# Windowed attention with sinks and a highway layer: x transposed by TensorE one block behind, weights loaded early, another order of the engines' work

## Chip, cores and metric

The kernel runs on one core of a Trainium2 chip. The metric is the device time of one execution in microseconds. The profile is one profiled execution of the kernel; its span runs from the first to the last instruction, and the execution's time is a little longer than the span.

## What is computed

Sliding-window attention that also keeps four sink positions, then a highway layer on its output:

```
scores = q k^T / sqrt(64)                 # 4 batches, 8 heads, 768 positions
keep   = (position < 4) or (0 <= i - j < 128)
a      = softmax(scores where keep)
x      = (a v), heads side by side        # 3072 tokens x 512
H      = max(x w_h, 0)
T      = sigmoid(x w_t + b_t)
out    = T H + (1 - T) x                  # 3072 x 512, float32
```

The inputs and the output are float32 in memory; the kernel computes in float16 with float32 accumulation.

## The kernel before, in words

**Tiling.** The 3072 tokens are 24 blocks of 128, six to a batch. A block sees its own 128 keys, those of the block before it in its batch, and the batch's four sinks. Block n goes through these steps, each a small function:

- `load_qk`, `load_v` (L79, L88): q, k, v of the block for all eight heads, by DMAs that GpSimd issues and that convert to float16.
- `pe_T`, `act_T`: TensorE transposes q and k (eight transposes into one PSUM tile `tp`), ScalarE copies them to SBUF (`qk`).
- `pe_S`, `act_S`, `dve_mask`: scores in two groups of four heads (g = 0 and 1), ScalarE's exponential (`e`), VectorE's product with the mask.
- `pe_sink`, `act_sink`: for two blocks at a time, the scores against the sinks and their exponential (`es`).
- `pe_A`: attention times v into one PSUM tile `av`; a column of v holds the softmax denominator. `dve_rec`, `dve_x`: its reciprocal and x (`xh`).
- x transposed, either by TensorE with a copy by ScalarE (`pe_X`, `act_X`) or by a DMA that SyncE issues (`sp_X`), into `xT`.
- the highway: `pe_Mt` (bias and x w_t, five matmuls), `act_u` (tanh), `pe_Mh` (x w_h, four matmuls), then VectorE's `dve_d`, `dve_e`, `dve_o` (`dd`, `ee`, `otok`), and SyncE's store of the block's 256 KB.

**Order.** No scheduler moves anything: the order of the calls in one loop is the order on each engine. Iteration i computes the attention product of block i, the scores of block i + 1, the transposes of block i + 2, the loads of block i + 10, x's transpose by TensorE of block i - 1 (for blocks up to 14; from 15 on SyncE's DMA, issued as soon as x is there), and the highway of block m = i - 4 (LAG is 4), whose VectorE part, o = i - 5, follows one iteration later. After block 23's attention the loop therefore runs on with highways alone. An engine that waits at one of its instructions holds all that stand behind it.

**PSUM.** The tag "m" has two buffers, taken in turn by `tp`, `xtp`, `tps`, `hps` and `sk`. The order of these in the loop decides which one's reader must be done before the next may be written: in the old order `tps` takes the buffer of `tp`, and `hps` that of `xtp`.

**Buffers in SBUF.** q, k have eight, v a ring of twelve. x and its transpose have LAG + 3 = 7.

**GpSimd's queue.** It issues the loads of blocks 0 to 2 and builds the masks, then the load of the first batch's four sink values of v (`load_sink_v(0)`), then, in iteration -2, copies the sinks' keys (`pool_sink`), spreads the sinks' values over a block-diagonal tile (`sink_v`, a product that waits for that load), and issues blocks 3 to 8, with the highway's weights behind blocks 4 and 5. For each later batch `pool_sink` and `sink_v` stand where its first block has been transposed.

Of the kernel before, what the change touches and what calls it, by code (L numbers as in the profile page):

```python
# [20 lines left out]
def kernel(  # L21
# [18 lines left out]
    nc = tc.nc  # L40
    P = 128

    B, H, S, D = q.shape
    NSINK = int(n_sink)
# [7 lines left out]
    NSC = S // P  # L52
    assert NSC % 2 == 0
    NB = NT // P
    NHP = H // 2
# [1 line left out]
    SCALE = 1.0 / math.sqrt(D)  # L57
    VW = H * 65 + 64
    AHEAD = 8
    LAG = 4  # L60
    WAT = 4

    const = ctx.enter_context(tc.tile_pool(name="const", bufs=1))
    sd_pool = ctx.enter_context(tc.tile_pool(name="p_sd", bufs=AHEAD))
    qkT_pool = ctx.enter_context(tc.tile_pool(name="p_qkT", bufs=5))
    e_pool = ctx.enter_context(tc.tile_pool(name="p_e", bufs=5))
    r_pool = ctx.enter_context(tc.tile_pool(name="p_r", bufs=3))
    x_pool = ctx.enter_context(tc.tile_pool(name="p_x", bufs=LAG + 3))
    td_pool = ctx.enter_context(tc.tile_pool(name="p_td", bufs=3))
    o_pool = ctx.enter_context(tc.tile_pool(name="p_o", bufs=4))  # L70
    s_ps = ctx.enter_context(tc.tile_pool(name="ps_s", bufs=2, space=bass.MemoryType.PSUM))
# [1 line left out]
    m_ps = ctx.enter_context(tc.tile_pool(name="ps_m", bufs=2, space=bass.MemoryType.PSUM))  # L73

    NV = AHEAD + 4
    v_ring = [const.tile([P, VW], FP16, tag=f"v{i}", name=f"v{i}") for i in range(NV)]
    qk_sd = {}

    def load_qk(n):  # L79
        b, c = divmod(n, NSC)  # L80
        rows = slice(c * P, (c + 1) * P)
        qsd = sd_pool.tile([P, H, D], FP16, tag="qsd", name="qsd")
        ksd = sd_pool.tile([P, H, D], FP16, tag="ksd", name="ksd")
        nc.gpsimd.dma_start(out=qsd, in_=q[b, :, rows, :].transpose([1, 0, 2]))  # L84
        nc.gpsimd.dma_start(out=ksd, in_=k[b, :, rows, :].transpose([1, 0, 2]))  # L85
        qk_sd[n] = (qsd, ksd)

    def load_v(n):  # L88
# [16 lines left out]
    wh_sb = const.tile([P, NOC, DM], FP16, tag="wh")  # L105
    wt_sb = const.tile([P, NOC, DM], FP16, tag="wt")
    bt32 = const.tile([1, DM], FP32, tag="bt32")
    bt16 = const.tile([P, DM], FP16, tag="bt16")
    ones_row = const.tile([P, P], FP16, tag="ones_row")
    NS4 = H * 4  # L110
    KW = NHP * P + 32
    ks_bd = [const.tile([P, KW], FP16, tag=f"ks{i}", name=f"ks{i}") for i in range(2)]
    vs_bd = [const.tile([P, H, 65], FP16, tag=f"vs{i}", name=f"vs{i}") for i in range(2)]
    vs_dn = [const.tile([NS4, D], FP16, tag=f"vd{i}", name=f"vd{i}") for i in range(2)]
# [9 lines left out]
            init_v(vt)  # L124

    def load_sink_v(b):
        nc.gpsimd.dma_start(out=vs_dn[b % 2], in_=v[b, :, 0:4, :])

    def sink_v(b):
        nc.gpsimd.tensor_tensor(  # L130
            out=vs_bd[b % 2][0:NS4, :, 0:D], in0=vs_dn[b % 2].unsqueeze(1).to_broadcast([NS4, H, D]),
            in1=bm[0:NS4, :].unsqueeze(2).to_broadcast([NS4, H, D]), op=ALU.mult)

    with tc.manual_schedule(engines={ENG.Pool}):
        load_qk(0)
        nc.gpsimd.affine_select(
            out=ident, in_=ident, compare_op=ALU.is_equal, fill=0.0,
            base=0, pattern=[[-1, P]], channel_multiplier=1)
        load_v(0)
        load_qk(1)  # L140
        nc.gpsimd.affine_select(
            out=mask[:, 1, :], in_=mask[:, 1, :], compare_op=ALU.is_ge, fill=0.0,
            base=0, pattern=[[1, P]], channel_multiplier=-1)
        load_v(1)
        nc.gpsimd.affine_select(
            out=mask[:, 0, :], in_=mask[:, 0, :], compare_op=ALU.is_ge, fill=0.0,
            base=-1, pattern=[[-1, P]], channel_multiplier=1)
        load_qk(2)
        nc.gpsimd.affine_select(
            out=bm, in_=bm, compare_op=ALU.is_ge, fill=0.0,  # L150
            base=0, pattern=[[-4, H]], channel_multiplier=1)
        nc.gpsimd.affine_select(
            out=bm, in_=bm, compare_op=ALU.is_ge, fill=0.0,
            base=3, pattern=[[4, H]], channel_multiplier=-1)
        load_v(2)
        load_sink_v(0)

    nc.sync.dma_start(out=bt32, in_=moe_b_t.unsqueeze(0))

    def more_constants():  # L160
# [3 lines left out]
        for i in range(2):  # L164
            nc.vector.memset(ks_bd[i], 0.0)
            nc.vector.memset(vs_bd[i], 0.0)
            nc.vector.memset(es_t[i], 0.0)

    def late_constants():
        nc.vector.tensor_copy(out=mask0, in_=mask[:, 1, :])  # L170
        nc.vector.memset(mask0[0:NSINK, :], 1.0)
        nc.vector.tensor_copy(out=mask1, in_=mask)
        nc.vector.memset(mask1[0:NSINK, 0, :], 1.0)
        nc.vector.tensor_scalar_mul(bt16[0:1, :], bt32, 0.5)

    def sink_ones():
        for i in range(2):
            nc.vector.tensor_scalar_mul(vs_bd[i][0:NS4, :, D:D + 1],
                                        bm[0:NS4, :].unsqueeze(2), 2.0)

# [3 lines left out]
            nc.tensor.matmul(w, lhsT=warm[:, 0:P], rhs=warm, start=True, stop=True)  # L184

    qkT, tp_of, s_of, e_of, av_of, rec_of = {}, {}, {}, {}, {}, {}
    xtp_of = {}
    xh_of, xT_of, t_of, u_of, h_of, dd_of, ee_of, sk_of = {}, {}, {}, {}, {}, {}, {}, {}

    def pe_T(n):  # L190
        qsd, ksd = qk_sd.pop(n)
# [7 lines left out]
    def act_T(n):  # L199
        qk = qkT_pool.tile([P, 2 * NHP, P], FP16, tag="qk", name="qk")  # L200
        nc.scalar.copy(out=qk, in_=tp_of.pop(n))  # L201
        qkT[n] = (qk[:, 0:NHP, :], qk[:, NHP:2 * NHP, :])

    def pool_sink(b):
        _, kT = qkT[b * NSC]
        ks = ks_bd[b % 2]
        for hh in range(2):
            rows = slice(64 * hh, 64 * hh + 64)
            dst = ks[rows, 0:NHP * 136].rearrange("p (a b) -> p a b", b=136)
            nc.gpsimd.tensor_copy(out=dst[:, :, 4 * hh:4 * hh + NSINK],  # L210
                                  in_=kT[rows, :, 0:NSINK])

    def pe_sink(n):
# [124 lines left out]
    def dve_d(n):  # L338
        dd = td_pool.tile([P, DM], FP16, tag="dd", name="dd")
        nc.vector.scalar_tensor_tensor(out=dd, in0=h_of.pop(n), scalar=0.0, in1=xh_of[n],  # L340
                                       op0=ALU.max, op1=ALU.subtract)
        dd_of[n] = dd
# [10 lines left out]
                                       op0=ALU.mult, op1=ALU.add)  # L353
        nc.sync.dma_start(out=out[n * P:(n + 1) * P, :], in_=otok)

    def by_dma(n):
        return n >= 15

    def on(n):
        return 0 <= n < NB  # L360

    with tc.manual_schedule(engines={ENG.PE, ENG.DVE, ENG.Activation, ENG.SP, ENG.Pool}):
        for i in range(-2, NB + LAG + 1):
            m, o = i - LAG, i - LAG - 1
            if i == -2:
                warm_up(8)
                more_constants()
                late_constants()
                sink_ones()
            if on(i) and i % NSC >= 2 and i % 2 == 0:  # L370
                act_sink(i)
            if on(i + 1):
                pe_S(i + 1, 0)
                act_S(i + 1, 0)
                pe_S(i + 1, 1)
            if on(o):
                dve_d(o)
            if on(i):
                dve_mask(i, 1)
            if on(i + 2):  # L380
                pe_T(i + 2)
            if on(i - 1) and not by_dma(i - 1):
                pe_X(i - 1)
            if on(o):
                dve_e(o)
            if on(i):
                pe_A(i)
            if on(i + 2):
                act_T(i + 2)
            if on(i - 1) and not by_dma(i - 1):  # L390
                act_X(i - 1)
            if on(i + 1):
                act_S(i + 1, 1)
                dve_mask(i + 1, 0)
            if on(i):
                dve_rec(i)
            if on(o):
                dve_o(o)
            if on(i):
                dve_x(i)  # L400
                if by_dma(i):
                    sp_X(i)
            if on(m):
                pe_Mt(m)
                act_u(m)
                pe_Mh(m)
            if on(i + 1) and (i + 1) % NSC >= 2 and (i + 1) % 2 == 0:
                pe_sink(i + 1)
            if on(i + 2) and (i + 2) % NSC == 0:
                pool_sink((i + 2) // NSC)  # L410
                sink_v((i + 2) // NSC)
            for n in (range(3, AHEAD + 1) if i == -2 else [i + 2 + AHEAD]):
                if n < NB:
                    load_qk(n)
                    load_v(n)
                if n == WAT:
                    nc.gpsimd.dma_start(out=wt_sb, in_=moe_w_t.rearrange("(kc p) of -> p kc of", p=P))
                if n == WAT + 1:
                    nc.gpsimd.dma_start(out=wh_sb, in_=moe_w_h.rearrange("(kc p) of -> p kc of", p=P))
            b = i // NSC + 1  # L420
            if i >= 0 and i % NSC == 1 and b < B:
                load_sink_v(b)


# [33 lines left out]
```

The softmax here doesn't subtract the row's maximum and nothing guards it: scores larger than these inputs give would overflow.

## Time and profile before

| what | us |
|---|---|
| median of 8 runs (lowest, highest) | 140.16 (138.28, 141.6) |
| the profiled execution | 139.09 |
| its span | 137.4 |
| TensorE busy | 114.0 |
| VectorE busy | 98.2 |
| ScalarE busy | 94.1 |
| GpSimd busy | 74.9 |
| start of the attention product of blocks 1, 2, 3, 4, 5 | 21.36, 26.07, 30.87, 35.96, 40.10 |
| first highway matmul | 37.00 |
| last attention product ends | 120.6 |
| last store issued | 133.47 |

How to read it: PE is TensorE's matmuls, PEld its weight loads, DVE is VectorE, ACT ScalarE, POOL GpSimd, SP SyncE. A group of instructions is named by its line, engine and operation, then the tile it writes, an arrow, and the tiles it reads. Busy time on TensorE is rough, since matmuls overlap and their ends are modelled: a matmul of 512 columns shows 379 ns while the next starts after 215 ns. "Idle before" is the time an engine stood before an instruction, with what released it. The chain of waits follows the work that ended last back to its beginning.

### The profile page before, as it was taken

The page shows a single profiled execution, that of the slowest core. Times are in us where ns is not written, and L with a number is a line of the kernel's source. Part 1 is how long each engine was busy: PE and PEld are TensorE (multiplying, and loading weights), DVE is VectorE, ACT ScalarE, POOL GpSimd, SP SyncE. Part 2 cuts the span into 40 slices and gives each one's busy share as a digit, 9 for nine tenths or more (in the row PEclk, how much of TensorE's full clock was granted, in tenths as well). Part 3 has the DMA queues.
Part 4 walks back from the last instruction along what each step waited for, and adds up shares of the span by engine and source line. Part 5 has one row for each costly group of instructions (what it writes and reads, how often), then busy time and mean ns, then how long its engine had stood idle before and what let it go on. Part 6 is the DMA issues. An engine that isn't in the chain of part 4 may idle for free.

```text
span 137.4 us, 3217 instructions
## 1 busy us (share of the span) xinstructions
PE 114.0 (83%) x1276; PEld 73.7 (54%) x1276; DVE 98.2 (72%) x213; ACT 94.1 (68%) x120; POOL 74.9 (55%) x99
## 2 busy tenths in 40 slices
PE   6747419946799799999997999999999999799910
PEld 2226319835676367567664675676655777354300
DVE  6434602364378697788789977978899988979970
ACT  3048807859687897897879878978697987413300
POOL 6994899955999949997799995005000000000000
PEclk9985555699999999999999999999999999999997
DMA  0999099999999999999999999943233243333322
GB/s 5 111 126 103 5 111 142 143 177 173 156 154 157 196 198 183 141 169 196 190 179 162 174 173 170 166 117 115 93 105 94 58 119 115 99 109 102 127 102 79
DMA packets 84626, 18.19 MB, mean 132 GB/s; under 512 B 80514, under 2 KB 81538, under 8 KB 84611
## 3 DMA queue, kind: packets, MB, share of 16 engines
q0 software_dynamic: 76256, 10.51, 113.5%
q1 hardware_dynamic: 8354, 7.48, 16.7%
q8 instruction: 10, 0.16, 0.5%
q14 instruction: 6, 0.04, 0.1%
HBM read 21.01 MB, written 6.29 MB: 199 GB/s over the span
## 4 chain that ended last, share of the span: by engine, by line
PE 44%; ACT 17%; POOL 15%; DMA 9%; DVE 8%; issue 3%; POOLq 0%; DVEq 0%
PE hps L334 11%; PE tps L321 11%; ACT e L249 9%; ACT qk L201 7%; DMA ksd<-in_k_dram 7%; PE av L275 5%; POOL qsd L84 5%; PE sps L241 4%; PE tps L319 4%; POOL ksd L85 4%; POOL v L92 4%; DVE dd L340 3%; DVE ee L346 3%; DVE otok L352 3%; PE sk L219 2%
## 5 line engine op out<-in xcount | busy, mean ns | idle before, releaser
L249 ACT ACTIVATE e<-sps,ebias 128x1024 f16<-128x1024 f32 (+1 forms) x48 | 49.8, 1045 | 6.4 <-PE sps L241 6.2
L260 DVE TENSOR_TENSOR e<-e,mask 128x1024 f16<-128x1024 f16 (+1 forms) x48 | 31.0, 646 | 5.5 <-ACT e L249 5.1
L201 ACT COPY qk<-tp 128x1024 f16<-128x1024 f16 x24 | 24.1, 1004 | 14.1 <-PE tp L196 14.1
L275 PE MATMUL av<-v,e 128*128 128x112 f16 x352 | 24.7, 219 | 0.8 <-DVE e L260 0.8
L340 DVE SCALAR_TENSOR_TENSOR dd<-hps,xh 128x512 f16<-128x512 f32 x24 | 16.6, 690 | 11.8 <-PE hps L334 11.7
L334 PE MATMUL hps<-wh_sb,xT 128*128 128x512 f16 x96 | 24.6, 379 | 0.0
L321 PE MATMUL tps<-wt_sb,xT 128*128 128x512 f16 x96 | 24.6, 379 | 0.0
L84 POOL DMA_DIRECT2D qsd<-in_q_dram x24 | 22.3, 928 | 3.6 <-DMA wt_sb<-in_moe_w_t_dram 1.6
L85 POOL DMA_DIRECT2D ksd<-in_k_dram x24 | 21.9, 912 | 2.3 <-DMA wh_sb<-in_moe_w_h_dram 1.5
L92 POOL DMA_DIRECT2D v<-in_v_dram x24 | 21.9, 912 | 2.0 <-DMA ksd<-in_k_dram 1.4
L275 PEld LDWEIGHTS <-e 128*128 128x128 f16 x352 | 21.3, 101 | 1.9 <-DVE e L260 1.2
L327 ACT ACTIVATE u<-tps 128x512 f16<-128x512 f32 x24 | 14.5, 603 | 10.6 <-PE tps L321 10.6
L241 PE MATMUL sps<-qk 64*128 64x128 f16 x352 | 15.9, 229 | 4.3 <-ACT qk L201 2.6
L346 DVE SCALAR_TENSOR_TENSOR ee<-u,dd 128x512 f16<-128x512 f16 x24 | 17.3, 721 | 0.5
L241 PEld LDWEIGHTS <-qk 64*128 64x128 f16 x352 | 11.1, 99 | 11.5 <-issue 9.5
L294 DVE TENSOR_TENSOR xh<-av,rec 128x512 f16<-128x512 f32 x24 | 16.4, 684 | 0.2
L321 PEld LDWEIGHTS <-xT 128*128 128x128 f16 x96 | 9.3, 97 | 13.0 <-issue 3.9
L352 DVE SCALAR_TENSOR_TENSOR otok<-xh,ee 128x512 f32<-128x512 f16 x24 | 15.6, 652 | 0.2
L334 PEld LDWEIGHTS <-xT 128*128 128x128 f16 x96 | 9.4, 98 | 11.8 <-issue 0.8
L194 PE MATMUL tp<-ident,qsd 128*128 128x128 f16 x96 | 10.4, 236 | 4.5 <-DMA qsd<-in_q_dram 4.5
L289 DVE RECIPROCAL rec<-av 128x8 f32<-128x8 f32 x24 | 4.9, 204 | 11.7 <-PE av L275 6.3
L196 PE MATMUL tp<-ident,ksd 128*128 128x128 f16 x96 | 10.2, 234 | 3.4 <-DMA ksd<-in_k_dram 3.4
(48 smaller groups left out, 93.7 us busy)
## 6 DMA issues: line engine op xcount, KB each, us to landing
out_dram<-otok SPq DMA_DIRECT2D x24, 256.0 KB, 2.6
qsd<-in_q_dram POOLq DMA_DIRECT2D x24, 128.0 KB, 6.8
ksd<-in_k_dram POOLq DMA_DIRECT2D x24, 128.0 KB, 6.7
v<-in_v_dram POOLq DMA_DIRECT2D x24, 128.0 KB, 6.6
wt_sb<-in_moe_w_t_dram POOLq DMA_DIRECT2D x1, 512.0 KB, 8.1
wh_sb<-in_moe_w_h_dram POOLq DMA_DIRECT2D x1, 512.0 KB, 9.9
xT<-xh SPq DMA_TRANSPOSE x9, 2.4
vd<-in_v_dram POOLq DMA_DIRECT2D x4, 4.0 KB, 7.0
```

The costliest lines, as they stand in the source:

```text
L84: nc.gpsimd.dma_start(out=qsd, in_=q[b, :, rows, :].transpose([1, 0, 2]))
L85: nc.gpsimd.dma_start(out=ksd, in_=k[b, :, rows, :].transpose([1, 0, 2]))
L92: nc.gpsimd.dma_start(out=vt[:, :, 0:D], in_=v[b, :, rows, :].transpose([1, 0, 2]))
L201: nc.scalar.copy(out=qk, in_=tp_of.pop(n))
L241: nc.tensor.matmul(sps[:, hh, o:o + P], lhsT=kk[rows, hp, :], rhs=qT[rows, hp, :], start=True, stop=True)
L249: nc.scalar.activation(out=e.rearrange("p a b c d -> p a (b c d)"), in_=sps[:, :, 0:2 * np_ * P], func=AF.Exp, bias=ebias, scale=SCALE)
L260: nc.vector.tensor_tensor(out=ev, in0=ev, in1=m.unsqueeze(1).to_broadcast([P, 4, np_ * P]), op=ALU.mult)
L275: nc.tensor.matmul(av[:, g, 2 * hl + hh, 0:_AVN], lhsT=e[:, hh, hl, pc, :], rhs=vt[:, 65 * h:65 * h + _AVN], start=first, stop=False, skip ...
L321: nc.tensor.matmul(tps, lhsT=xT[:, kc, :], rhs=wt_sb[:, kc, :], start=False, stop=(kc == NOC - 1))
L334: nc.tensor.matmul(hps, lhsT=xT[:, kc, :], rhs=wh_sb[:, kc, :], start=(kc == 0), stop=(kc == NOC - 1))
L340: nc.vector.scalar_tensor_tensor(out=dd, in0=h_of.pop(n), scalar=0.0, in1=xh_of[n], op0=ALU.max, op1=ALU.subtract)
L346: nc.vector.scalar_tensor_tensor(out=ee, in0=u_of.pop(n), scalar=1.0, in1=dd_of.pop(n), op0=ALU.add, op1=ALU.mult)
```

## The change

- x of every block but 14 to 21 is transposed by TensorE (before: blocks 0 to 14), in the iteration after its attention; blocks 14 to 21 by SyncE's DMA.
- The highway of a block runs one iteration after its attention, or two where the DMA transposes it. Iteration 15 has none, iteration 23 has two (21 and 22). The loop ends two iterations after the last block instead of five.
- Inside an iteration, x's transpose and ScalarE's copy of it come directly behind the next block's scores; ScalarE's copy of q, k follows, ahead of the exponential of the second score group.
- The first iterations (-2 to 1) have an order of their own: scores and transposes are put at the end of the iteration, and the highway of block 0 ahead of the transposes of block 2.
- GpSimd issues the weights behind v of block 1, ahead of q, k of block 2. The sinks' values of batch 0 are spread by VectorE in iteration 0; those of later batches by GpSimd, with the load issued a batch ahead.
- x and its transpose have five buffers.

The diff, cut to its core:

```diff
-    LAG = 4
-    WAT = 4
...
-    x_pool = ctx.enter_context(tc.tile_pool(name="p_x", bufs=LAG + 3))
+    x_pool = ctx.enter_context(tc.tile_pool(name="p_x", bufs=5))
...
+    XBAR = range(14, 22)
...
-    def sink_v(b):
-        nc.gpsimd.tensor_tensor(
+    def sink_v(b, eng):
+        eng.tensor_tensor(
...
+    def load_w(w, sb):
+        nc.gpsimd.dma_start(out=sb, in_=w.rearrange("(kc p) of -> p kc of", p=P))
...
-        load_v(1)
         nc.gpsimd.affine_select(
             out=mask[:, 0, :], in_=mask[:, 0, :], compare_op=ALU.is_ge, fill=0.0,
             base=-1, pattern=[[-1, P]], channel_multiplier=1)
-        load_qk(2)
+        load_v(1)
+        load_sink_v(0)
+        load_w(moe_w_t, wt_sb)
+        load_w(moe_w_h, wh_sb)
...
+        load_qk(2)
         load_v(2)
-        load_sink_v(0)
+        load_qk(3)
...
-    def by_dma(n):
-        return n >= 15
+    def lag(n):
+        return 2 if n in XBAR else 1
+
+    def highway(i):
+        return [m for m in range(NB) if m + lag(m) == i]
+
+    def has_sink(n):
+        return on(n) and n % NSC >= 2 and n % 2 == 0
...
-        for i in range(-2, NB + LAG + 1):
-            m, o = i - LAG, i - LAG - 1
+        for i in range(-2, NB + 2):
+            ms, os_ = highway(i), highway(i - 1)
             if i == -2:
                 warm_up(8)
                 more_constants()
-                late_constants()
-                sink_ones()
...
-            if on(i + 1):
+            if i >= 2 and on(i + 1):
                 pe_S(i + 1, 0)
                 act_S(i + 1, 0)
                 pe_S(i + 1, 1)
-            if on(o):
-                dve_d(o)
+            if on(i - 1) and i - 1 not in XBAR:
+                pe_X(i - 1)
+                act_X(i - 1)
+            for o in os_:
+                if o not in dd_of:
+                    dve_d(o)
             if on(i):
                 dve_mask(i, 1)
-            if on(i + 2):
+            if i >= 2 and on(i + 2):
                 pe_T(i + 2)
-            if on(i - 1) and not by_dma(i - 1):
-                pe_X(i - 1)
-            if on(o):
+                act_T(i + 2)
+            if i >= 2 and on(i + 1):
+                act_S(i + 1, 1)
+            for o in os_:
                 dve_e(o)
             if on(i):
                 pe_A(i)
-            if on(i + 2):
-                act_T(i + 2)
-            if on(i - 1) and not by_dma(i - 1):
-                act_X(i - 1)
-            if on(i + 1):
-                act_S(i + 1, 1)
+            if i >= 2 and on(i + 1):
                 dve_mask(i + 1, 0)
             if on(i):
                 dve_rec(i)
-            if on(o):
+            for o in os_:
                 dve_o(o)
             if on(i):
                 dve_x(i)
-                if by_dma(i):
+                if i in XBAR:
                     sp_X(i)
-            if on(m):
+            for m in ms:
                 pe_Mt(m)
                 act_u(m)
                 pe_Mh(m)
-            if on(i + 1) and (i + 1) % NSC >= 2 and (i + 1) % 2 == 0:
+            if i == 1:
+                dve_d(0)
+                pe_T(2)
+                act_T(2)
+            if -1 <= i < 2:
+                for g in range(2):
+                    pe_S(i + 1, g)
+                    act_S(i + 1, g)
+                dve_mask(i + 1, 0)
+            if i < 2:
+                n = {-2: 0, -1: 1, 1: 3}.get(i)
+                if n is not None:
+                    pe_T(n)
+                    act_T(n)
+            if has_sink(i + 1):
                 pe_sink(i + 1)
+            if i == 0:
+                sink_ones()
+                sink_v(0, nc.vector)
             if on(i + 2) and (i + 2) % NSC == 0:
-                pool_sink((i + 2) // NSC)
-                sink_v((i + 2) // NSC)
-            for n in (range(3, AHEAD + 1) if i == -2 else [i + 2 + AHEAD]):
+                b = (i + 2) // NSC
+                pool_sink(b)
+                if b:
+                    sink_v(b, nc.gpsimd)
+                if b + 1 < B:
+                    load_sink_v(b + 1)
+            for n in {-2: range(3, AHEAD + 1), 0: [], 1: [10, 11]}.get(i, [i + 2 + AHEAD]):
                 if n < NB:
-                    load_qk(n)
+                    if n > 3:
+                        load_qk(n)
                     load_v(n)
-                if n == WAT:
-                    nc.gpsimd.dma_start(out=wt_sb, in_=moe_w_t.rearrange("(kc p) of -> p kc of", p=P))
-                if n == WAT + 1:
-                    nc.gpsimd.dma_start(out=wh_sb, in_=moe_w_h.rearrange("(kc p) of -> p kc of", p=P))
-            b = i // NSC + 1
-            if i >= 0 and i % NSC == 1 and b < B:
-                load_sink_v(b)
```

More of the change, by code (lines that the diff above doesn't have):

```diff
@@ L75 @@
     NV = AHEAD + 4
+    NS4 = H * NSINK
+    KW = NHP * P + 32
+    XBAR = range(14, 22)
     v_ring = [const.tile([P, VW], FP16, tag=f"v{i}", name=f"v{i}") for i in range(NV)]
@@ L109 @@
     ones_row = const.tile([P, P], FP16, tag="ones_row")
-    NS4 = H * 4
-    KW = NHP * P + 32
     ks_bd = [const.tile([P, KW], FP16, tag=f"ks{i}", name=f"ks{i}") for i in range(2)]
@@ L126, in load_sink_v @@
     def load_sink_v(b):
-        nc.gpsimd.dma_start(out=vs_dn[b % 2], in_=v[b, :, 0:4, :])
-    def sink_v(b):
-        nc.gpsimd.tensor_tensor(
+        nc.gpsimd.dma_start(out=vs_dn[b % 2], in_=v[b, :, 0:NSINK, :])
+    def sink_v(b, eng):
+        eng.tensor_tensor(
             out=vs_bd[b % 2][0:NS4, :, 0:D], in0=vs_dn[b % 2].unsqueeze(1).to_broadcast([NS4, H, D]),
             in1=bm[0:NS4, :].unsqueeze(2).to_broadcast([NS4, H, D]), op=ALU.mult)
+    def load_w(w, sb):
+        nc.gpsimd.dma_start(out=sb, in_=w.rearrange("(kc p) of -> p kc of", p=P))
     with tc.manual_schedule(engines={ENG.Pool}):
@@ L147 @@
             base=-1, pattern=[[-1, P]], channel_multiplier=1)
-        load_qk(2)
+        load_v(1)
+        load_sink_v(0)
+        load_w(moe_w_t, wt_sb)
+        load_w(moe_w_h, wh_sb)
         nc.gpsimd.affine_select(
             out=bm, in_=bm, compare_op=ALU.is_ge, fill=0.0,
-            base=0, pattern=[[-4, H]], channel_multiplier=1)
+            base=0, pattern=[[-NSINK, H]], channel_multiplier=1)
         nc.gpsimd.affine_select(
             out=bm, in_=bm, compare_op=ALU.is_ge, fill=0.0,
-            base=3, pattern=[[4, H]], channel_multiplier=-1)
+            base=NSINK - 1, pattern=[[NSINK, H]], channel_multiplier=-1)
+        load_qk(2)
         load_v(2)
-        load_sink_v(0)
+        load_qk(3)
     nc.sync.dma_start(out=bt32, in_=moe_b_t.unsqueeze(0))
@@ L167, in more_constants @@
             nc.vector.memset(es_t[i], 0.0)
-    def late_constants():
         nc.vector.tensor_copy(out=mask0, in_=mask[:, 1, :])
@@ L186 @@
     qkT, tp_of, s_of, e_of, av_of, rec_of = {}, {}, {}, {}, {}, {}
-    xtp_of = {}
-    xh_of, xT_of, t_of, u_of, h_of, dd_of, ee_of, sk_of = {}, {}, {}, {}, {}, {}, {}, {}
+    xtp_of, xh_of, xT_of, t_of, u_of, h_of, dd_of, ee_of, sk_of = {}, {}, {}, {}, {}, {}, {}, {}, {}
     def pe_T(n):
@@ L209, in pool_sink @@
             dst = ks[rows, 0:NHP * 136].rearrange("p (a b) -> p a b", b=136)
-            nc.gpsimd.tensor_copy(out=dst[:, :, 4 * hh:4 * hh + NSINK],
+            nc.gpsimd.tensor_copy(out=dst[:, :, NSINK * hh:NSINK * hh + NSINK],
                                   in_=kT[rows, :, 0:NSINK])
@@ L367 @@
                 more_constants()
-                late_constants()
-                sink_ones()
-            if on(i) and i % NSC >= 2 and i % 2 == 0:
+            if has_sink(i):
                 act_sink(i)
-            if on(i + 1):
+            if i >= 2 and on(i + 1):
                 pe_S(i + 1, 0)
```

## The prediction, made before the changed kernel ran

> **What bounds the kernel now.** The profiled execution took 139.09 us: a span of 137.4 and 1.7 around it. The median of the eight runs is 140.16, 1.07 above this execution, so I sum against 139.09 and add 1.07 at the end. I read the page's slices first, then the chain of waits in time order, then busy time in stretches that I cut where the chain changes character.
>
> The slices (40 of 3.4 us each):
>
> ```profile
> PEclk9985555699999999999999999999999999999997
> DMA  0999099999999999999999999943233243333322
> ```
>
> Slice 4 (13.7 to 17.2 us) has no DMA at all in the middle of a phase that waits for loads, and TensorE's granted clock is halved from about 10 to 26 us. The chain, times from the span's start, then length:
>
> ```profile
> 11.25 2.87 DMA vd<-in_v_dram
> 14.29 1.03 POOL vs L130
> ...
> 25.52 9.93 DMA ksd<-in_k_dram
> ...
> 77.22 0.91 ACT qk L201
> 78.17 0.38 PE tps L319
> 78.55 0.86 PE tps L321 x4
> 79.41 0.86 PE hps L334 x4
> 80.27 0.51 PE sk L219 x8
> 80.83 0.35 issue
> 81.18 1.09 ACT e L249
> 82.27 0.90 ACT qk L201
> 83.21 0.38 PE tps L319
> ...
> 130.63 0.69 DVE otok L352
> 131.32 0.61 DVE dd L340
> 132.03 0.70 DVE ee L346
> 132.75 0.69 DVE otok L352
> ```
>
> Three regimes. To 36 us the chain is GpSimd issuing loads (about 0.9 us each) and the loads themselves; GpSimd stands 2.87 us for the small sink load and then works 1.03 us before it issues q of block 3. From 36 to 118 us it alternates between TensorE and ScalarE: the highway's first matmul waits until ScalarE has evacuated q, k (they share a PSUM tag of two buffers), and behind the highway stand the next scores. At the end VectorE runs dd, ee, otok alone, 2.12 us a block. The stretches (length, then busy time of PE, PEld, DVE, ACT, POOL, granted clock, DMA share, GB/s):
>
> ```profile
> 14.00:16.00 2.00, 1.24 (x19) 0.86 (x16) 1.35 (x3) 2.00 (x3) 1.71 (x2) 0.50 0.00 0
> 36.00:81.00 45.00, 42.67 (x521) 27.93 (x519) 35.97 (x67) 38.55 (x52) 41.09 (x52) 1.00 2.09 173
> 81.00:118.00 37.00, 36.78 (x457) 24.33 (x452) 32.62 (x63) 31.83 (x41) 5.01 (x8) 1.00 0.69 115
> 118.00:137.40 19.40, 12.07 (x67) 5.36 (x64) 13.84 (x22) 3.45 (x6) 0.00 (x0) 0.95 0.32 109
> ```
>
> TensorE is the nearest bound in the middle and is poorly used at both ends.
>
> **What the Trainium skill says.** "Perfetto Trace Analysis", section Optimization Strategy: where the most contended engine changes over time, interleaving the regimes may pay. The trace has such regimes, as shown. "DMA: Bandwidth & Descriptors", section on the anatomy of a SWDGE DMA: each DMA costs some 2 us however small; the sink load took 2.87 us to land, so waiting for it is never cheap. "TensorE: Matmul & The Clock Gate", section What's actually happening: half clock until about 3.4 us of sustained activity. The trace agrees loosely: full clock came at about 26.2 us, after 5.7 us without a gap, and held through 28 to 36 us, where TensorE was busy 4.58 of 8 us. "SBUF — State Buffer", section Who interferes with whom: a VectorE operation with two SBUF inputs and a GpSimd operation that reads SBUF block each other; here an ee that ran beside GpSimd's vs product took 1.53 us against 0.69.
>
> **The change, part by part.**
>
> *Start, loads.* GpSimd's wait (2.46 us idle) and product (1.03) go: up to 3.5 us of issuing are freed. In exchange both weights (512 KB each as stored) are issued ahead of q, k of block 2. Issue times from the rows (0.9 a load, 0.8 a weight, 0.6 the sink load): v of block 1 is issued by 7.8 us, wt and wh by 10, k of block 2 by 12.2. The first six loads ran at 127 GB/s (mean of 3 to 12 us), the backlogged phase from 22 to 36 us at 162. By about 10 us 768 KB are in; another 1.05 MB of weights plus 0.26 MB take 8 us: q, k of block 2 land at about 18.5 instead of 12, block 4's k at about 22.8 instead of 25.2, block 5's at 25.2 instead of 30.4. Weights alone are not shown as a stream; at 195 (best 2 us window) or 127 GB/s wh lands between 16 and 19 us.
>
> *Start, compute.* The scores of block 1 come ahead of T of block 2, so A of block 1 runs at about 14 to 16 us (before 21.3: it stood behind T of block 3). Behind it stand Mt(0) and Mh(0), at half clock 2.1 and 1.7 us: to 19.6. Only then T of block 2 (queued behind the weights' landing on TensorE: T(2), S(2), T(3), the sinks). At full clock: T 0.5, copy 1.0, two exponentials 2.1, copy of T(3) 0.9, sinks 0.6, exponentials 1.5, so A(2) at about 26.7, T(4) without a wait, A(3) near 31, A(4) 35.6, A(5) 40.3; before 26.07, 30.87, 35.96, 40.10. The start gains nothing in time (+0.2), but by A(5) four highways are done instead of one. Bounds: if the weights land early, or the old 3.5 us come whole, -3; if the clock stays half to block 3, the 6 us of TensorE work from T(2) to Mh(1) double and part is hidden: +4.
>
> *Middle, count.* From A(5) to the end of A(23) the old kernel runs 18 highways on TensorE, the new one 17: 1.94 us less (0.22 + 0.86 + 0.86). Iteration 15 has none, so VectorE (3.9 us an iteration with dd, ee, otok) holds it there: I take -1.5. Transposes of blocks 22 and 23 move from SP to TensorE, that of 14 to SP: 0.23 us on PE and 0.59 on ACT each, one in the middle either way.
>
> *Middle, order.* From Mt to Mt, iterations 4 to 14 took 50.6 us. Their TensorE work at issue pace (chain: S 0.55, T 0.55, X 0.23, A 1.02, highway 1.94, sink 0.55, less where a block has no predecessor or sink) sums to 46.6. So 4.0 us are waits, most of them Mt on ScalarE's q, k copy and scores on exponentials. Now x's transpose and its copy come first: Mt needs ScalarE's x copy (about 1.95 us into the iteration: exponential to 1.46, copy 0.5), while A ends at 2.36; Mh needs the q, k copy at 2.85, while Mt ends at 3.44. Both waits should vanish. ScalarE paces at about 4.05, VectorE at 3.8 to 3.9. I take half of it, -2.2; bounds +1.5 and -4.
>
> *Tail.* A(23) ended at 120.6, the last otok at 133.44: 12.84. Now after A(23): highways 21 and 22 on PE (Mh(22) waits for dd(21), because they share a PSUM buffer) to +4.0, X(23) to +4.4, its copy +4.95, Mt +5.9, Mh +6.75; VectorE meanwhile is full with dd, ee, otok of 21 and 22 until +7.4, then those of 23: +9.5. -3.3. The last store takes its 3.96 us as before.
>
> *Taken at zero.* The sink product of batch 0 on VectorE (not shown; GpSimd's took 1.03, take 0.7) falls where VectorE idled 5.85 us, and its load lands by 12 us; uncovered it costs those 0.7. On GpSimd's queue the ks copies (0.5) and the sink load of batch 1 (0.6) now stand ahead of v of block 3; with the product gone there the queue is still some 3 us ahead of before, and later batches' products find loads that landed long ago (they idled 0.2 us together before). Transposes on SP: landed in 2.4 us, needed two iterations later, 7 us. Stores begin at 27 instead of 42 us, beside the loads: four of 256 KB by 40 us, some 6 us of DMA time; covered, since block 5 lands 5 us ahead of need; otherwise up to 1.5 us per block. Five x buffers for lives of at most four iterations: no wait.
>
> Sum: +0.2 - 1.5 - 2.2 - 3.3 = -6.8. Span 130.6, execution 132.3, median **133.4**.
>
> **Rivals.** *The start takes it back* (0.20): weights ahead of block 2 starve TensorE, A(5) comes at 43.5 (+3.2), and half of the order's gain is lost (+1.2): 137.8. For it: block 2 lands 6 us later and the 9.93 us wait shows that loads decide there. Against: the same bytes had to come before A(5) anyway. *The chain inside the iteration* (slower, 0.12): with a lag of one block VectorE's x, TensorE's X, ScalarE's copy and Mt must follow one another, and T, A, Mt stand behind X on TensorE. x ends barely 0.6 us before X is due; if VectorE runs one pair (otok, xh: 1.3) late, TensorE idles 0.7 in each of 13 iterations: +9.1 against -6.8, 142.5. It decides from 0.52 us per iteration. Against: x to x through the next A is 0.68 + 0.23 + 0.55 + 1.02 + 0.2 + 0.65 = 3.3 us, under the 4.3 us period. *All of it works* (0.06): order's gain 4.0, start -2: 129.4. *It doesn't do what it says*: the ring's back-pressure (GpSimd idled 1.6 and 1.5 us for the weights before) replaces the sink wait; that is inside the first rival.
>
> **Numbers.** Forecast 0.62 (131 to 136). The range 130 to 139.5 takes in the first rival and leaves out most of the last and the slower one, 0.17. A measurement of this kernel tells about 1% from nothing, below 138.76 or above 141.56. Faster: 0.62 + 0.06 + two thirds of 0.20; same 0.08, slower 0.12.
>
> **What would show it.** Right: no DMA-free slice near 14 us; first highway by 20 us; A(5) within 2 us of 40; Mt no longer released by ScalarE's q, k copy; the last otok 9 to 10 us after A(23). Wrong: TensorE idle before X or Mt in every iteration, released by VectorE's xh or ScalarE's xT; half clock beyond 30 us; T(2) to T(5) still waiting for loads.

## The result and the profile after

The changed kernel takes 133.57 us in the median (132.6 to 134.67, 11 runs), the kernel before 139.8 beside it (32 runs): a ratio of 0.959 with a 95% interval of 0.956 to 0.962. This ratio and those below leave out runs more than 1.5% above the fastest of the same kernel, so they are not simply the quotients of the medians. The forecast was 133.4 us and faster. Its profiled execution took 133.66 us with a span of 131.9, against 139.09 and 137.4: 5.4 us less, 5.5 in the span.

The slices of the changed kernel:

```profile
PEclk9999999959999999999999999999999999999995
DMA  0999999999999999999999999934143324422042
```

The DMA-free slice is gone. TensorE's granted clock falls once while TensorE is at work, from 26.6 to 30.0 us. (The first clock record of this trace begins at 19.8 us; the digits 9 before it stand for no record, and the pace of the matmuls there was half.) The chain of waits of the changed kernel (start, length, what):

```profile
5.39 4.38 DMA ksd<-in_k_dram
...
16.76 1.71 PE tps L323 x4
18.47 1.58 PE hps L336 x4
20.05 0.22 PE tp L196 x4
...
73.72 0.48 ACT xT L315
74.25 0.38 PE tps L321
74.63 0.86 PE tps L323 x4
75.49 0.86 PE hps L336 x4
76.35 0.35 PE sps L243 x8
76.73 1.11 ACT e L251
...
126.41 0.61 DVE dd L342
127.12 0.70 DVE ee L348
127.84 0.69 DVE otok L354
```

In this execution no load stands in the chain from 10 us on. It runs through TensorE, and the first highway (tps and hps at 16.76, at half pace: 0.43 us a matmul instead of 0.215) stands ahead of the transposes of block 2, as forecast. Where the attention product is short, the first highway matmul now waits for x's copy (xT) instead of the longer one of q, k. At the end VectorE's three operations on a block (dd, ee, otok) stand only for the last blocks. The stretches of the changed kernel, to be held against those of the kernel before:

```profile
13.70:17.20 3.50, 2.72 (x19) 1.86 (x20) 2.44 (x7) 1.07 (x2) 2.95 (x4) 1.00 1.48 176
36.00:81.00 45.00, 43.64 (x538) 29.06 (x537) 38.29 (x71) 39.79 (x53) 38.35 (x48) 1.00 2.05 179
81.00:114.00 33.00, 32.56 (x429) 22.09 (x427) 28.59 (x55) 28.59 (x36) 1.42 (x3) 1.00 0.52 106
114.00:131.90 17.90, 11.06 (x90) 5.87 (x84) 12.15 (x21) 5.76 (x9) 0.00 (x0) 0.92 0.23 81
```

TensorE's idle time from 36 to 81 us went from 2.33 to 1.36 us only. The difference is clearer by milestones. This table is worked out from both timelines; a milestone is the first highway matmul of an iteration, which stands right behind that iteration's attention product (in iteration 15 of the changed kernel there is none).

| stage | before, us | after, us | difference |
|---|---|---|---|
| start to iteration 4 | 37.00 | 38.65 | +1.65 |
| iterations 4 to 14 | 46.21 | 44.93 | -1.28 |
| 14 to 16 | 9.10 | 7.37 | -1.73 |
| 16 to 23 | 28.28 | 28.28 | 0.00 |
| 23 to the last otok's end | 12.85 | 9.31 | -3.54 |
| to the end of the span | 3.96 | 3.40 | -0.56 |
| sum | 137.4 | 131.9 | -5.5 |

The same stages serve for the experiments. Each is read from one profiled execution; the first stage is the least certain, since the half pace at the start ended at 18.0 us in one of the later traces (`e4_sinkwait`) and at 19.8 us in the changed kernel's. Ratios below are to the kernel before, run beside them on the same chip.

### The profile page after: what moved, and what is told of

It reads as the page before. It is cut to its first block, busy times and chain, and to the rows that moved or that the text cites. A ratio compares the mean times of both kernels' runs of the same rounds, so it can differ in the third digit from the quotient of the medians.

```text
span 131.9 us, 3224 instructions
## 1 busy us (share of the span) xinstructions
PE 114.4 (87%) x1280; PEld 73.5 (56%) x1280; DVE 97.3 (74%) x214; ACT 94.4 (72%) x121; POOL 73.5 (56%) x98
## 4 chain that ended last, share of the span: by engine, by line
PE 55%; ACT 24%; DVE 8%; issue 5%; DMA 3%; POOL 3%; POOLq 0%; DVEq 0%
ACT e L251 13%; PE tps L323 12%; PE hps L336 12%; PE av L277 9%; ACT qk L203 7%; PE sps L243 7%; DMA ksd<-in_k_dram 3%; PE tps L321 3%; PE sk L221 3%; DVE dd L342 3%; PE tp L196 3%; PE tp L198 3%; ACT u L329 2%; PE av L283 2%; DVE e L262 2%
## 5 line engine op out<-in xcount | busy, mean ns | idle before, releaser
L277 PE MATMUL av<-v,e 128*128 128x112 f16 x352 | 25.7, 222 | 2.1 <-DVE e L262 2.1
L323 PE MATMUL tps<-wt_sb,xT 128*128 128x512 f16 x96 | 26.0, 395 | 0.0
L336 PE MATMUL hps<-wh_sb,xT 128*128 128x512 f16 x96 | 25.4, 388 | 0.0
L243 PE MATMUL sps<-qk 64*128 64x128 f16 x352 | 14.8, 223 | 2.9 <-ACT qk L203 2.6
L348 DVE SCALAR_TENSOR_TENSOR ee<-u,dd 128x512 f16<-128x512 f16 x24 | 16.3, 684 | 0.1
L336 PEld LDWEIGHTS <-xT 128*128 128x128 f16 x96 | 9.6, 100 | 12.0 <-issue 1.1
L243 PEld LDWEIGHTS <-qk 64*128 64x128 f16 x352 | 10.5, 97 | 9.8 <-issue 7.5
L323 PEld LDWEIGHTS <-xT 128*128 128x128 f16 x96 | 9.8, 102 | 10.9 <-issue 2.0
L321 PE MATMUL tps<-bt,ones_row 128*128 128x512 f16 x24 | 9.6, 401 | 0.8 <-DVE dd L342 0.6
L196 PE MATMUL tp<-ident,qsd 128*128 128x128 f16 x96 | 9.8, 227 | 0.4 <-DMA qsd<-in_q_dram 0.2
```

Of the source, the lines that this page charges most:

```text
L243: nc.tensor.matmul(sps[:, hh, o:o + P], lhsT=kk[rows, hp, :], rhs=qT[rows, hp, :], start=True, stop=True)
L277: nc.tensor.matmul(av[:, g, 2 * hl + hh, 0:_AVN], lhsT=e[:, hh, hl, pc, :], rhs=vt[:, 65 * h:65 * h + _AVN], start=first, stop=False, skip ...
L323: nc.tensor.matmul(tps, lhsT=xT[:, kc, :], rhs=wt_sb[:, kc, :], start=False, stop=(kc == NOC - 1))
L336: nc.tensor.matmul(hps, lhsT=xT[:, kc, :], rhs=wh_sb[:, kc, :], start=(kc == 0), stop=(kc == NOC - 1))
```

## The experiments

**The lag alone.** `e1_lag4` puts every highway four blocks back again and keeps the rest.

```diff
-        return 2 if n in XBAR else 1
+        return 4
...
-        for i in range(-2, NB + 2):
+        for i in range(-2, NB + 5):
...
             if i == 1:
-                dve_d(0)
                 pe_T(2)
```

> The changed kernel with a lag of four blocks for every highway again (seven x buffers, five iterations after the last block), all else as changed. Decomposition theory: the tail from the last highway matmul inside the loop to the last otok goes from 9.3 back to about 12.85 us (+3.5), the hole at iteration 15 is lost (+1.7), but the start has no highways in iterations 1 to 3 and reaches the attention product of block 5 some 3 to 4 us earlier: in all +1 to +2.5 us on the changed kernel, ratio to the kernel before 0.966 to 0.977. Rival, the short lag is the whole gain: ratio 0.99 to 1.0.

Measured: 0.979 (0.974 to 0.985). Span 134.9, 3.0 more than the changed kernel: start -2.66, iterations 4 to 14 -0.02, 14 to 16 +1.25, 16 to 23 0.00, tail +4.3. Every stage moved the way the theory has it, but none by its price: the start gained less than 3 to 4 us, the hole at iteration 15 was worth less than 1.7, and the tail, 0.8 over its price, carried the ratio a little past the range. The middle took 44.91 us with either lag, so its gain doesn't come from the lag. In the timeline TensorE stood 2.98 us for q of block 2, which started its transposes at 19.06: with the weights ahead, loads bound this start, and in the changed kernel the first highway hides that wait.

**Lag and weights together.** `f1_lag4_wlate` also puts the weights back behind blocks 4 and 5.

```diff
-        load_w(moe_w_t, wt_sb)
-        load_w(moe_w_h, wh_sb)
...
                     load_v(n)
+                if n == 4:
+                    load_w(moe_w_t, wt_sb)
+                if n == 5:
+                    load_w(moe_w_h, wh_sb)
```

> The lag of four of e1_lag4 with the weights issued behind blocks 4 and 5, so without the two parts of the change that belong together (short lag, early weights), but with its order inside an iteration and without GpSimd's wait. Theory that the short lag and the early weights pay for each other and little more: the attention product of block 5 comes some 3 us earlier than in e1_lag4 (40.5 to about 37.5), the rest as there: span about 132, ratio 0.957 to 0.968, close to the changed kernel. Rival, the lag is where the gain is: ratio over 0.975.

Measured: 0.963 (0.959 to 0.967), median 134.08 us, and a span of 131.9: not told apart from the changed kernel. Iteration 4 came at 33.02 us, 5.63 ahead of it, and the tail and iterations 14 to 16 gave exactly that back (+4.3, +1.25). So the short lag and the early weights, the largest part of the diff, pay for each other and for nothing more, as the changed kernel stands. Part of this balance is a stretch at half clock in the changed kernel's start; without it (`e3_warm`, below) the short lag comes out ahead.

**Weights alone.** `e8_wlate` moves the weights back as above, with the short lag kept.

> The changed kernel with the weights issued behind blocks 4 and 5 again, all else as changed. Theory that the short lag needs them early: TensorE stands at the first highway until wt and wh land, at about 24 and 28 us, with the transposes of block 2 behind it: +5 to +9 us on the changed kernel, ratio 0.995 to 1.023. Rival (first rival of the prediction), early weights starve block 2 and late ones help: ratio under 0.955.

Measured: 1.058 (1.049 to 1.068), past even the range. The timeline of `e8_wlate`, TensorE's matmuls (start, length, what, then the wait before):

```profile
25.97 1.86 PE L321 MATMUL tps<-wt_sb,xT 128*128 128x512 f16 x4 [9.24 <-DMA wt_sb<-in_moe_w_t_dram]
31.06 1.89 PE L334 MATMUL hps<-wh_sb,xT 128*128 128x512 f16 x4 [3.23 <-DMA wh_sb<-in_moe_w_h_dram]
32.74 0.63 PE L194 MATMUL tp<-ident,qsd 128*128 128x128 f16 x4
```

TensorE stood 12.5 us at the first highway with everything of block 2 behind it, and worked at half pace (four transposes 0.63 us, not 0.40) until about 42 us. The weights had to come early for the short lag; alone, either half is worse than both.

**GpSimd's wait, in the old kernel.** `e5_oldsink` is the kernel before with one edit: the first batch's sink product on VectorE at the end of iteration 0 (`sink_v` takes the engine as an argument).

```diff
-                sink_v((i + 2) // NSC)
+                if i >= 0:
+                    sink_v((i + 2) // NSC, nc.gpsimd)
+            if i == 0:
+                sink_v(0, nc.vector)
```

> The kernel before with one thing alone: the first batch's sink product on VectorE at the end of iteration 0, so that GpSimd doesn't wait for the sink load. Theory that the old start was set by the loads: the DMA-free stretch at 14 us goes and the attention products of blocks 2 to 4 come 2 to 3.5 us earlier: ratio 0.975 to 0.986. Rival, the hole was hidden (backlog of the weights): 0.995 to 1.0.

Measured: 0.975 (0.970 to 0.980). Span 133.4, 4.0 less than before, 3.8 of it ahead of iteration 4 (33.17 instead of 37.00; from there on 46.07, 9.10, 28.27 and 12.86 us, as before). TensorE's transposes of block 3, in the kernel before and then in `e5_oldsink`:

```profile
18.69 0.61 PE L194 MATMUL tp<-ident,qsd 128*128 128x128 f16 x4 [2.52 <-DMA qsd<-in_q_dram]
20.53 0.61 PE L196 MATMUL tp<-ident,ksd 128*128 128x128 f16 x4 [1.23 <-DMA ksd<-in_k_dram]
```

```profile
16.33 0.61 PE L194 MATMUL tp<-ident,qsd 128*128 128x128 f16 x4
16.73 0.63 PE L196 MATMUL tp<-ident,ksd 128*128 128x128 f16 x4
```

The two waits, 3.75 us together, are gone. The stretch of `e5_oldsink` that was empty in the kernel before, where the DMA moved 6 GB/s in it:

```profile
13.70:17.20 3.50, 2.74 (x33) 2.21 (x32) 2.90 (x6) 3.03 (x3) 3.50 (x5) 1.00 1.87 119
```

The 1.00 for the clock stands for no record here either (the first begins at 20.5 us); the pace was that of the kernel before, eight attention products in 0.95 us in both. Block 1's attention product came at 17.59 us against 21.36, so 3.77 us of the gain were there while both still ran at half pace: the loads are the cause, not the clock. A few lines bring over half of what the whole change brings.

**GpSimd's wait, in the changed kernel.** `e4_sinkwait` gives the product back to GpSimd, ahead of q, k of block 2.

```diff
                 sink_ones()
-                sink_v(0, nc.vector)
...
-                if b:
-                    sink_v(b, nc.gpsimd)
+                sink_v(b, nc.gpsimd)
+                if i == -2:
+                    load_qk(2)
+                    load_v(2)
+                    load_qk(3)
```

> The changed kernel with the first batch's sink product on GpSimd again, ahead of q, k of block 2, where it waits for its load. Theory that the start is now set by TensorE and by the weights: q, k of block 2 are issued about 2 us later, but the weights are still moving then and T of block 2 stands behind the first highway until 19.9 us: 0 to +0.7 us, ratio 0.958 to 0.965. Rival, GpSimd's wait is worth its 3.5 us as in the old start: +2.5 to +3.5 us, ratio 0.976 to 0.984.

Measured: 0.952 (0.945 to 0.959), below the range and not told apart from the changed kernel. GpSimd waited 0.51 us here, since the load had been issued ahead of the weights, and the product took 1.03; q of block 2 was issued 0.8 us later. So the product with its short wait costs nothing measurable in the new order. The full 2.5 us wait was not had here, and what it would cost was not tried. There is little slack left: in `e4_sinkwait` TensorE waited 0.42 us for k of block 2 at 20.16 us, and in `e2_order`, `e6_allpe`, `e7_xbar6` and `f3_T3_warm`, which leave the product on VectorE, 0.43 to 0.45 us. VectorE's share isn't free either: in the changed kernel the product (0.68 us) stands in the chain ahead of block 1's second mask, for which TensorE waited 0.41 us, and the first highway began at 16.13 us against 15.59 in `e4_sinkwait`.

**The order inside an iteration.** `e2_order` takes q, k ahead of x again on TensorE and on ScalarE.

```diff
-            if on(i - 1) and i - 1 not in XBAR:
-                pe_X(i - 1)
-                act_X(i - 1)
...
                 pe_T(i + 2)
                 act_T(i + 2)
+            if on(i - 1) and i - 1 not in XBAR:
+                pe_X(i - 1)
+                act_X(i - 1)
```

> The changed kernel with the old order inside an iteration: q, k transposed ahead of x on TensorE and copied ahead of x on ScalarE. Order theory: TensorE's first highway matmul waits for ScalarE's copies again (x's copy is now the second), 0.3 to 0.5 us in each of some 13 iterations: +1.3 to +5 us, ratio 0.968 to 0.995. Rival, the middle gained only by having one highway less there: no change, ratio 0.956 to 0.962.

Measured: 0.988 (0.983 to 0.994), with iterations 4 to 14 in 48.73 us: 3.8 more than the changed kernel and 2.5 more than the kernel before. One iteration in the chain of `e2_order`:

```profile
46.15 1.11 ACT e L251
47.26 0.90 ACT qk L203
48.16 0.50 ACT xT L315
48.66 0.05 issue
48.71 1.04 PE tps L323 x4
49.74 0.86 PE hps L336 x4
50.60 0.35 PE sps L243 x8
```

Exponential, both copies, highway, scores: 4.8 us a round, in series. With the old lag of four, x's copy wasn't needed in the same iteration. With a lag of one it is, and it stands last. So the new order is worth 1.3 us at a lag of four (46.21 us in the kernel before, 44.91 in `e1_lag4`), and 3.8 at a lag of one, where it is a condition. (The first figure also holds the sink loads issued a batch ahead, which no run takes apart.)

**The half clock.** `e3_warm` fills TensorE's wait for the q, k copy of block 3 with 28 idle matmuls, whose result the sink scores overwrite.

```diff
             qT, _ = qkT[n + t]
+            if n == 2 and t == 1:
+                for _ in range(28):
+                    nc.tensor.matmul(sk[:, 1, :], lhsT=warm[:, 0:P], rhs=warm[:, 0:P],
+                                     start=True, stop=True)
```

> The changed kernel with 28 idle matmuls of 128 columns in the 2.1 us in which TensorE waits for the q, k copy of block 3 (about 23 to 25 us); their result is overwritten by the sink scores. Clock theory: the half clock from about 26.8 to 30.3 us is brought on by that wait; it goes, and the attention product of block 3 comes 1.0 to 1.8 us earlier, ratio 0.945 to 0.952. Rival, the clock falls for another reason or the copies set the pace there: no change, ratio 0.957 to 0.962.

Measured: 0.944 (0.938 to 0.950), as the clock theory has it, just past its range. TensorE's timeline in the changed kernel:

```profile
25.11 0.38 PE L221 MATMUL sk<-qk,ks 128*128 128x128 f16 x4 [2.11 <-ACT qk L203]
26.68 0.95 PE L277 MATMUL av<-v,e 128*128 128x112 f16 x8
27.43 0.43 PE L283 MATMUL av<-vs,es 128*128 128x260 f16 x1
29.04 1.52 PE L323 MATMUL tps<-wt_sb,xT 128*128 128x512 f16 x4
```

and in `e3_warm`:

```profile
23.44 1.73 PE L222 MATMUL sk<-warm 128*128 128x128 f16 x28
26.99 0.56 PE L281 MATMUL av<-v,e 128*128 128x112 f16 x8
27.39 0.28 PE L287 MATMUL av<-vs,es 128*128 128x260 f16 x1
28.23 1.03 PE L327 MATMUL tps<-wt_sb,xT 128*128 128x512 f16 x4
```

The same eight products take 0.95 us after the wait and 0.56 without it. Iteration 4 came at 37.34 instead of 38.65, and all later stages were the same to 0.02 us, so the 1.3 us are that. All four runs of `e3_warm` (131.54 to 132.46 us) were shorter than every run of the changed kernel (132.6 and up), so the gain isn't one execution's.

The fall isn't bound to the wait in every execution. The same place in `e7_xbar6` and then in `e6_allpe`, whose starts are the same code:

```profile
25.10 0.59 PE L221 MATMUL sk<-qk,ks 128*128 128x128 f16 x4 [1.84 <-ACT qk L203]
27.84 0.95 PE L277 MATMUL av<-v,e 128*128 128x112 f16 x8
```

```profile
25.92 0.38 PE L221 MATMUL sk<-qk,ks 128*128 128x128 f16 x4 [1.84 <-ACT qk L203]
27.47 0.56 PE L277 MATMUL av<-v,e 128*128 128x112 f16 x8
```

The wait is the same, but one execution ran at half pace directly behind it and the other not at all; the changed kernel's fell only 1.5 us after the wait. Of five profiled executions with a wait of 1.8 to 2.1 us here, four fell (also `e2_order` and `e4_sinkwait`); of the four in which the wait was shortened to 0.9 us or less (`e3_warm` and the three with block 3's copy moved, below), none did. A single long wait isn't needed either: in `e5_oldsink` the pace was half from 27.3 to 30.7 us behind three waits of 1.03, 0.83 and 0.43 us. What decides in a given execution these traces don't show.

**A shorter wait.** `f2_T3early` moves block 3's transposes and copy ahead of the second exponential of block 2; `f3_T3_warm` adds 14 idle matmuls to it.

```diff
                     pe_S(i + 1, g)
+                    if i == 1 and g == 1:
+                        pe_T(3)
+                        act_T(3)
                     act_S(i + 1, g)
...
-                n = {-2: 0, -1: 1, 1: 3}.get(i)
+                n = {-2: 0, -1: 1}.get(i)
```

> The changed kernel with the transposes of block 3 and ScalarE's copy of them ahead of the second exponential of block 2 in iteration 1. TensorE's wait of 2.1 us there should be 1.1: clock theory -0.3 to -1.3 us on the changed kernel, ratio 0.947 to 0.957. Rival, ScalarE's sum sets the pace there: no change, 0.957 to 0.962.

> f2_T3early with 14 idle matmuls in what is left of the wait. Clock theory: TensorE at full pace from 20 us on, -1.3 to -2.2 us on the changed kernel, ratio 0.940 to 0.950, no slower than e3_warm. Rival: no better than f2_T3early.

Measured: 0.948 (0.944 to 0.953) and 0.943 (0.939 to 0.947), with medians of 131.97 and 131.41 us. In `f2_T3early` the wait was 0.88 us, the pace held, and iteration 4 came at 36.20. Both beat the changed kernel; whether the idle matmuls add to the earlier copy is within their intervals. The earlier copy does more than hold the pace: `e6_allpe`, which kept its pace without it, reached iteration 4 at 37.82; of the 1.6 us between them 0.7 were there at block 2's transposes already. With `e3_warm` these are the runs in which the short lag with early weights gains over `f1_lag4_wlate` (0.963), which was not run with such an edit.

**Which blocks the DMA transposes.** In `e6_allpe` none, in `e7_xbar6` blocks 6 to 21, in `f4_xbar15` (on top of `f3_T3_warm`) 15 to 22; only the line of XBAR is edited.

```diff
-    XBAR = range(14, 22)
+    XBAR = range(0)
```

> The changed kernel with all 24 transposes of x on TensorE and a lag of one throughout. TensorE-bound theory: blocks 14 to 21 cost 0.23 to 0.3 us each (+2.2), the iteration without a highway is gone (+1.7), the tail has one highway less (-2.1): +1 to +2.5 us on the changed kernel, ratio 0.966 to 0.978. Rival, VectorE sets the pace of those iterations and hides the transposes: no change or faster, ratio up to 0.960.

Measured: 0.979 (0.972 to 0.985), just past the range. By stages against the changed kernel: 14 to 16 +1.96, 16 to 23 +2.47 (forecast +1.7 and +2.2), tail -2.07 (-2.1), and the start -0.83, where the pace held. TensorE sets the pace of those iterations: it was busy 32.3 of the 33 us from 81 to 114 us, ScalarE, which got the copies, 29.6.

> The changed kernel with blocks 6 to 21 (instead of 14 to 21) transposed by SyncE's DMA, lag two. TensorE-bound theory: eight transposes of 0.23 us and eight copies leave TensorE and ScalarE: -1 to -2.5 us, ratio 0.941 to 0.952. Rival, a DMA transpose beside the loads lands late (over two iterations, some 8 us) or slows the loads, and the highway waits for it: +1 us or more, ratio over 0.966.

Measured: 0.970 (0.956 to 0.983), its four runs from 133.48 to 137.79 us: the theory's gain isn't there, and a loss isn't firm. The DMA issues of the changed kernel and then of `e7_xbar6` (count, median us to landing):

```profile
xT<-xh SPq DMA_TRANSPOSE x8, 2.5
```

```profile
xT<-xh SPq DMA_TRANSPOSE x16, 5.7
```

The 5.7 mixes two kinds: the transposes up to 85 us, beside the loads, landed in 7.0 to 8.4 us, the later ones in 2.9 (median). TensorE stood 3.8 us for three of them. All this is from the profiled execution, the longest of the four, so the rival's mechanism is seen, but its price isn't measured: here the DMA took transposes off TensorE cheaply only once the loads were through.

> f3_T3_warm with blocks 15 to 22 instead of 14 to 21 transposed by SyncE's DMA: block 22's transpose leaves TensorE ahead of the last attention product, highways 22 and 23 stand together behind block 23's transpose. Theory that the tail is set by the order of TensorE's and VectorE's work behind the last attention product: TensorE no longer waits between Mh(22), x's transpose and copy, and Mt(23); last otok 8.7 instead of 9.3 us after it, -0.3 to -1 us on f3_T3_warm, ratio 0.934 to 0.941. Rival, VectorE's nine operations bound the tail: no change, 0.940 to 0.946.

Measured: 0.956 (0.950 to 0.962), median 133.44: slower than `f3_T3_warm`, and neither theory had that. The iteration without a highway moved to 16, where it saves less (14 to 17 took 12.61 instead of 11.38 us), and from iteration 23 to the last otok it took 10.07 instead of 9.31: with highways 22 and 23 back to back, VectorE does ee and otok of both behind the last matmul. The theory's premise failed too: TensorE still waited 0.56 us for dd between x's transpose and the next highway, so the wait was not taken away, and what it is worth was not tested.

## Why the prediction came out right, and where it didn't

The number was right (133.57 against 133.4) and the direction too. The steps behind it were right to different degrees, and some of the agreement is luck: the sum was -6.8 us and the profiled executions differ by 5.4. The median of the kernel before lay 1.07 above its profiled execution, that of the changed kernel 0.09 below its own. By ratio I forecast 0.952 and it is 0.959. (Below, T(n), S(n), A(n) and X(n) are block n's q, k transposes, scores, attention product and x's transpose, Mt and Mh the two halves of its highway.)

- **Start, +0.2 forecast, +1.65 measured** at iteration 4, +1.88 at A(5) (41.98 against 40.10), just inside the 2 us of 40 that I had named as a sign. A(2) began at 26.68 us, as worked out (26.7), with luck in the working: the steps I listed add up to 26.2, and the last, 1.5 us of exponentials, wasn't in the way; TensorE's own S(3), X(1) and T(4) were (1.4 us). Mis-sized was the clock: I took it at full from 20 us on, with +4 as the bound, and in the profiled execution it fell again behind a 2.1 us wait that stood in my own list (the copy of T(3) behind two exponentials). `e3_warm` gives 1.3 us for it. On GpSimd's queue the copies of the sinks' keys and the second sink load ran from 9.93 us, ahead of q of block 2 and not behind k of block 3 as I read the code. So the order of the calls isn't quite the order on this queue; in the kernel before, too, these copies (9.58 us) ran ahead of v of block 2. No cost of it is seen here. And 127 GB/s was the mean of 6 to 12 us; from 3 to 12 it was 116.
- **"Up to 3.5 us of issuing are freed", at no gain.** The start did gain nothing, and this step hides most. `e5_oldsink` shows that the same 3.5 us are worth 4.0 of span in the old order. In the new one the weights, issued ahead of block 2, take about as much (`e1_lag4` reaches iteration 4 2.97 us later than `f1_lag4_wlate`, which issues them late), for three more highways by A(5). `e4_sinkwait` delayed q of block 2 by only 0.8 us and lost nothing; whether the new order could do without the whole 3.5 us is open.
- **Count, -1.5 forecast, -1.73 measured** between iterations 14 and 16, with VectorE's part carried over as described; 16 to 23 didn't move. The agreement is in part luck: with a lag of four and a highway in every iteration, `e1_lag4` and `f1_lag4_wlate` took 8.62 us there, so the missing highway is worth 1.25 us. The other 0.48 came with the order and with block 14's transpose, which left TensorE.
- **Order, -2.2 forecast, -1.28 measured** in iterations 4 to 14. (My 50.6 and 46.6 us are for eleven iterations, to Mt of 15; the stage has ten.) Mt no longer waited for the q, k copy, as forecast, but TensorE's own work did not become the pace everywhere: where A is short Mt still waits for x's copy, as the chain at 73.72 shows, and with a sink TensorE waited for ScalarE's tanh (0.6 us in all). The mechanism was right, the size too large. What I missed is that the order and the short lag aren't two terms to be added: `e2_order` loses 3.8 us.
- **Tail, -3.3 forecast, -3.54 measured**, 9.31 us against my +9.5. The last store landed 0.56 us sooner, which I had at zero.
- **Taken at zero.** The sink product on VectorE took 0.68 us (0.7 forecast) and did not quite hide: TensorE waited 0.41 us for the mask behind it. GpSimd's wait for the weights shrank to 0.99 us (before 1.6 and 1.5). DMA transposes landed in 2.5 us. Stores beside the loads delayed none of block 3 to 6's transposes.
- **Rivals.** *The start takes it back* was near in mechanism: `f1_lag4_wlate` is 5.6 us ahead at iteration 4, so early weights and early highways do cost the start that. But the tail and the hole at iteration 15 return it. *The chain inside the iteration* didn't come by VectorE's x, as I had it; it exists on ScalarE and is what `e2_order` ran into.

What stays open: what decides whether the clock falls behind the wait (four profiled executions of five), how much of the run-to-run spread it makes, and what GpSimd's full wait would cost in the new order.

## What to carry to other kernels

Before pricing a rewrite, take its smallest edit alone: here moving one small product off the queue that issues the loads gave 2.5% of the 4.1%, while the shorter lag and the earlier loads, most of the code, only paid for each other until the half clock behind them was dealt with. A shorter pipeline lag moves work from the tail to the start, so it pays only where the start has idle time that loads leave free, and it turns copies that were far from due into links of a chain; their order has to change with it. About two microseconds of waiting on TensorE, in one piece or several, can cost another one after it, at half pace; here shortening the wait, or filling it, was worth 1.3 us.

## What the runs showed of the hardware

- After a 2.1 us wait TensorE's matmuls ran at half pace from 26.6 to 30.0 us (eight products 0.95 instead of 0.56 us). After a 1.84 us wait at the same place they did so in one execution (`e7_xbar6`) and not in another (`e6_allpe`). The half-clock stretches behind these waits were 3.4 us long in four traces (the changed kernel, `e2_order`, `e4_sinkwait`, `e5_oldsink`) and 6.8 in `e7_xbar6`.
- The changed kernel's trace has no clock record before 19.8 us, and its page shows the full clock there, while its matmuls ran at half pace (0.43 us for 512 columns at 16 to 18 us). The pace of like instructions is the better witness.
- A DMA transpose of 128 x 512 landed in 2.5 us (median) once GpSimd's loads were through, and in 7.0 to 8.4 us beside them in `e7_xbar6`.
